# A two-layer transformer kernel: finer loads and a new order in the preamble, and step 0 by halves, in place of an earlier softmax turn in even steps, earlier rows of the second chain and a held-back tile load

## The chip, the cores and the metric

One core of one Trainium2 chip. The metric is the device time of one execution in microseconds; less is better. Three runs of the kernel before gave 1550.05, 1551.38 and 1552.74 us, median 1551.38 us.

## The reference

The input x (1 x 2048 x 448, bf16) goes through two identical layers, with the same weights both times. A layer is a recurrent attention and then a gated feed-forward net (FFN), each behind a layer norm without gain and added to its input:

```
x = x + A(layernorm(x), mem0, Wq, Wk, Wv, Wo)        # 16 heads of 256
x = x + B(layernorm(x), W_gate, W_up, W_down)        # 448 -> 1792 -> 448, relu(gate) * up
(both once more)

A: for each of 64 segments of 32 rows:
    h = concat(mem, xs)                              # 8 + 32 rows
    q, k, v = h Wq, h Wk, h Wv                       # per head
    p = softmax(mask(q k^T / 16))
    o = sum over heads of (p v) Wo
    mem = o[:8]; out rows = o[8:]
```

The 64 segments are a chain: segment s+1 needs the memory rows that segment s left.

## The kernel before, in words

**Two chains.** Layer 1 is chain C1, layer 2 is chain C2; C2 runs six segments (LAG) behind. There are 70 steps. Step g does segment g of C1 and g-6 of C2: steps 0 to 5 hold C1 alone (`single`), steps 6 to 63 hold both (`dual`), steps 64 to 69 hold C2 alone. The 29 even and 29 odd dual steps differ in how their values are gathered: an odd one takes C1's values of x from the step before it, an even one computes them for both chains.

**Folded weights.** The kernel does not form q, k, v. A preamble folds the weights: M = Wk Wq^T per head (`make_M`, 4 heads a call, into `M_sb` and `MT_sb`) and B = Wv Wo per head (`make_B`, 2 heads a call, into `B_sb` and `BT_sb`). For M, Wk and Wq come in transposed by the DMA (`load_T`, line 166, 1024 columns or four heads at a time, 0.92 MB each). For B, Wv comes plain (`load_vo`, lines 177 and 178, 512 columns), TensorE turns it (`turn_B`), and Wo comes plain (line 180). The last two calls, make_B(6) and make_B(7), are made inside step 0. `place(h)` puts heads of even j in the first half of the four-slot groups of `B_sb`, and heads of odd j in the second; so the first part (x = 0) of a `Values` object needs only even j, its second part only odd j.

**A step.** `GPhase` forms G = M h^T in PSUM banks ("gps", evicted by ScalarE and VectorE at line 474). From G come the scores ("S_ps"), then the softmax on VectorE, ScalarE and GpSimd, with its results `Px` and `Pm`. TensorE turns these (`turn_P`, transposes into "PT_ps", copies at line 805). In between `Values` forms h B for the memory (`vm`) and for x (`vx`): a call `both(False)` issues the matmuls over the first 384 features, `both(True)` the tails over the last 64, and whichever comes second ends the sums and evicts them (line 407). The last matmuls ("AT_ps") weigh the values; their first 8 rows per chain are turned ("mps") and become the memory columns of the next step.

**The FFN** of a 128-row tile is cut into ten pieces, queued per chain, and dropped into the steps by `fill` at the hooks inG, mid, before, end and last. The first piece, `turn`, brings the normed rows in turned form to `xnT`, by a DMA transpose (line 315) in dual steps. The normed rows themselves (`rows`, lines 267 and 270, tiles xd_90 and xd_91) are made in `turn` for C1, right behind the first eviction of G by VectorE (`recent["G1"]`). For C2 they are made at the end of the step before, behind the last sum of another tile (`recent["sum"]`, line 349), for the 13 tiles 1 to 13; tile 0 and the tail go C1's way. C1's tiles start in steps with g % 4 = 0, C2's in steps with g % 4 = 2.

**x tiles** live in a ring of six. When C2's FFN has ended a tile, it is stored (line 351), and the tile six further on is queued in `x_next` and loaded by `load_x` (line 366) in the mid hook of a later step.

**Order.** A planner orders instructions by priority and its own costs, but `in_order` ties all TensorE work, and the preamble's loads on SP's queue, to program order. `behind` ties a single instruction behind another on its engine. One PSUM pool of 8 banks, one tag, serves every PSUM tile of the kernel. Buffers of the preamble come in pairs (wk, wq, wv, wo; two tiles wvn).

Of the kernel before, what the change touches and what calls it, by code (L numbers as in the profile page):

```python
# [9 lines left out]
BF = mybir.dt.bfloat16  # L10
# [41 lines left out]
def build_kernel(ctx, tc, A_x, A_mem0, A_Wq, A_Wk, A_Wv, A_Wo, B_W_gate, B_W_up, B_W_down, out,  # L52
# [9 lines left out]
    glob = ctx.enter_context(tc.tile_pool(name="glob", bufs=1))  # L62
    R = min(6, ntiles)
    x_ring = glob.tile([P, R, DM], BF)
    nc.sync.dma_start(x_ring[:, 0:2, :], x_dram[0:256].rearrange("(t p) d -> p t d", p=P))

    def xsl(t):
        return x_ring[:, t % R, :]
# [48 lines left out]
    def in_order(op):  # L117

        eng = op.ins.engine
        if eng in last_of:  # L120
            tc.add_manual_dep(op.ins, last_of[eng],
                              mybir.DependencyInfo(mybir.DependencyClass.NoSync, mybir.DependencyReason.DATA),
                              reason="in_order")
        last_of[eng] = op.ins.name
# [36 lines left out]
    srcs = {n: w.rearrange("d h e -> d (h e)") for n, w in (("k", A_Wk), ("q", A_Wq), ("v", A_Wv))}  # L161
    WoF = A_Wo.rearrange("h (t p) d -> p (h t) d", p=P)

    def load_T(n, i):
        t = bp.tile([P, 8, DM], BF, tag=f"w{n}", name=f"w{n}")
        in_order(nc.sync.dma_start_transpose(t[:], srcs[n][:, 1024 * i:1024 * (i + 1)]))  # L166
        return t

    kq, vo = {}, {}

    def load_kq(i):
        kq[i] = load_T("k", i), load_T("q", i)

    def load_vo(j):

# [53 lines left out]
                              wn[:, dc, 128 * (2 * a + b):128 * (2 * a + b) + 128], ident[:])  # L229
            copy_out(wv[:, 2 * a:2 * a + 2, :], tp[:, :, 0:DM])  # L230

    def make_B(j):

        wv, wo = wv_T.pop(j), vo.pop(j)[1]
        for hh in range(2):
            for mt in range(3):
                ps = psum.tile([P, 512], F32, tag="ps")
                product(ps[:, 0:DM], wv, wo, hh, 128 * mt, 128)
                copy_out(B_sb[:, mt, place(2 * j + hh), :], ps[:, 0:DM], j == 7)
        ps = psum.tile([P, 512], F32, tag="ps")  # L240
        for e, half in enumerate(HALVES):
            product(ps[half, 0:DM], wv, wo, e, 384, 64)
        copy_out(BT_sb[:, place(2 * j), :], ps[:, 0:DM], j == 7)
# [13 lines left out]
    def ln_rows(st, twice=False, after=None):  # L257

        xt, mv, rstd = st
        if twice:  # L260
            xd = xds[n_xn[1] % 2]
            dst, xt = xd[:, :, 0], xt.rearrange("p (k d) -> p k d", d=64)
        else:
            xd = xns[n_xn[0] % 2]
            n_xn[0] += 1
            dst = xd[:, 0:DM]
        behind(nc.vector.tensor_scalar(out=dst, in0=xt, scalar1=mv[:, 0:1], scalar2=rstd[:],
                                       op0=ALU.subtract, op1=ALU.mult), after)
        if twice:
            nc.vector.tensor_copy(xd[:, :, 1], xd[:, :, 0])  # L270
        else:
            nc.vector.tensor_copy(xd[:, DM:DMP], xd[:, 384:DM])
        return xd
# [28 lines left out]
    class FFN:  # L302
# [4 lines left out]
        def norm(self):  # L307
            self.stats = ln_stats(self.t, recent.get("hh"))

        def rows(self, after):  # L310
            self.xn = ln_rows(self.stats, True, after)
            self.xnT = late_sb["xnT"][n_xn[1] % 2]
            n_xn[1] += 1
            if recent["two"]:
                nc.sync.dma_start_transpose(self.xnT[:], self.xn[:].rearrange("p k a b -> p (k a b)"))

        def turn(self):
            if self.xn is None:
                self.rows(recent["G1"])
            if not recent["two"]:  # L320
                tps = psum.tile([P, NCH, P], BF, tag="ps", name="tps")
                for k in range(NCH):
                    transpose(tps[:, k], self.xn[:, k].rearrange("p a b -> p (a b)"), ident[:])
                nc.scalar.copy(self.xnT[:], tps[:])
            self.hh = late_sb["fb"].tile([P, FT, P], BF, tag="hh", name="hh")
# [14 lines left out]
        def down(self, lo, hi):  # L340
            if lo == 0:
                self.dps = psum.tile([P, 512], F32, tag="ps", name="dps")
            ps = self.dps
            for f in range(lo, hi):
                matmul(ps[:, 0:DM], self.hh[:, f, :], late_sb["Wd"][:, f, :], start=(f == 0), stop=(f == FT - 1))
            if hi < FT:
                return
            xt = xsl(self.t)
            recent["sum"] = nc.vector.tensor_tensor(xt, ps[:, 0:DM], xt, op=ALU.add)
            if self.c is C2:  # L350
                nc.sync.dma_start(out_dram[self.t * 128:(self.t + 1) * 128, :], xt)
                t2 = self.t + R
                if t2 < ntiles:
                    x_next.append(t2)

        def pieces(self):
            yield from [self.turn] + [lambda f=f: self.gate_up(f) for f in range(0, FT, 2)] 
            yield from [lambda: self.down(0, 7), lambda: self.down(7, FT)]

    ffn_q = {0: deque(), 1: deque()}  # L360
    x_next = deque()

    def load_x():
        while x_next:
            t = x_next.popleft()
            nc.sync.dma_start(xsl(t), x_dram[t * 128:(t + 1) * 128, :])

    def fill(cid, n):
        for _ in range(n):
# [194 lines left out]
    def single(g, c, inG, mid, soft, before, late, end, last):  # L564
# [67 lines left out]

        alone = g + 1 < LAG if c is C1 else g + 1 < nsteps and (g + 1 - c.lag) % 4 != 0
        soft()
        if not g:
            vm.both(True)
        vm.both(False)
        if odd:
            vox = prev_vom[0]
            v = ahead[g + 1] = x_values(g + 1) if alone else None  # L640
        else:
            v = ahead.pop(g, None)
            if v is None:
                v = x_values(g)
                v.part(0, False)
                v.part(0, True)
            v.part(1, True)
            vox = v.dst
        prev_vom[0] = VOm
        before()  # L650
# [68 lines left out]
    def dual(g, chains, inG, mid, soft, before, late, end, last):  # L719
# [90 lines left out]
        if len(vx) == 2:  # L810
            vx[0].both(False)
            before()
            turn_P()
            vx[0].both(True)
            vx[1].both(True)
            vx[1].both(False)
        else:
            vx[0].part(0, False)
            vx[0].both(True)
            before()  # L820
            turn_P()
            vx[0].part(1, False)
# [59 lines left out]
    def none():  # L882
        pass

    def make_two(j):
        turn_B(j)
        turn_B(j + 1)
        for i in (j, j + 1):
            make_B(i)
            load_vo(i + 2)  # L890

    load_vo(0)
    load_vo(1)
    load_kq(0)
    make_two(0)
    load_kq(1)
    make_M(0)
    tps0 = transposed(mem_in, MEM)
    nc.vector.tensor_copy(mem0T[:], tps0[:, :, 0:MEM])
    set_mem0(C1)  # L900
    for t in range(2):
        prep_stats(C1, t)
        prep_rows(C1, t)
        prep_pe(C1, t)
    make_two(2)
    load_kq(2)
    make_M(1)
    load_kq(3)
    make_two(4)
    if R > 2:  # L910
        in_order(nc.sync.dma_start(x_ring[:, 2:R, :], x_dram[256:R * 128].rearrange("(t p) d -> p t d", p=P)))
    first_G.append(GPhase(0))
    for i in range(2):
        first_G[0].quarter(i)
    make_M(2)
    first_G[0].quarter(2)
    make_M(3)
# [3 lines left out]
    for g in range(nsteps):  # L921
        gb, r = divmod(g, 4)
        if g == LAG:
            set_mem0(C2)
        inG = mid = soft = before = late = end = last = none
        if g == 0:
            def mid():
                turn_B(6)
                turn_B(7)
                make_B(6)  # L930

            def soft():
                make_B(7)
                late_pools()
        elif r == 0:
            def inG():
                fill(0, 1)

            def mid():
                fill(0, 2)  # L940

            def end():
                fill(0, 1)

            def last():
                fill(0, 1)
        elif r == 1:
            def inG():
                prep_stats(C1, gb + 2, recent["G"])

            def mid():
                prep_rows(C1, gb + 2, recent["G"])
                fill(0, 2)

            def before():
                fill(0, 3)
                prep_stats(C2, gb - 1)
                prep_rows(C2, gb - 1)

            def end():  # L960
                prep_pe(C1, gb + 2)
                fill(1, 1)
                prep_pe(C2, gb - 1)

            def last():
                fill(1, 1)
        elif r == 2:
            def inG():
                fill(1, 1)

            def mid():
                fill(1, 1)

            def end():
                fill(1, 1)

            def last():
                fill(1, 1)
        else:
            def mid():  # L980
                fill(1, 1)
                load_x()

            def before():
                fill(1, 1)

            def end():
                fill(1, 1)

            def last():  # L990
                fill(1, 1)
        step(g, inG, mid, soft, before, late, end, last)
        for c in (C1, C2):
            t, j = divmod(g - c.lag, 4)
            if j == 3 and 0 <= t < ntiles:
                f = FFN(c, t)
                f.norm()
                if c is C2 and recent["two"] and g + 1 < nseg and t:
                    f.rows(recent["sum"])
                ffn_q[c.cid].extend(f.pieces())  # L1000
    fill(1, 20)

# [52 lines left out]
```

## Time and profile before

| | |
|---|---|
| Median of 3 runs | 1551.38 us |
| The profiled execution: time, span | 1551.38 us, 1549.6 us |
| Granted TensorE clock, mean | 0.999 |
| TensorE (PE) busy | 1515.6 us, 98% |
| VectorE (DVE), ScalarE (ACT), GpSimd (POOL) busy | 910.5, 625.7, 148.2 us |
| Step 0 begins (mask matmul) | 65.47 us |
| Step 1's first G matmul | 83.50 us |
| Chain that ended last | 92% PE, 2% DMA, 2% DVE, 2% SP's queue |

Times in the profile are microseconds from the span's start unless marked ns. "PEld" is TensorE loading weights, "SPq" a DMA issue on SP's queue. In a line of the timeline stand the start, the duration, engine, source line, operation, out<-in and count. A DMA's issue is not its landing.

### The profile page before, as it was taken

To read this page: it belongs to the slowest core of one execution; us is meant where nothing else is said; L and a number is where in the kernel's file an instruction comes from. 1 tells how busy PE (TensorE), PEld (TensorE's weight loads), DVE (VectorE), ACT (ScalarE), POOL (GpSimd) and SP (SyncE) were. 2 spreads that over 40 slices of the span, in tenths; PEclk is the share of its full clock that TensorE was granted. 3 is DMA by queue.
4 is the path that set the end of the run, shared out by engine and by line. 5 is a ranking of instruction groups with operands and counts; after the bars stand their busy time and mean duration, and the time that the engine had idled before them with its cause. 6 is when DMAs were issued, how large, how long until landed. Compare 5 with 4: busy or idle time off the path is not lost.

```text
span 1549.6 us, 82294 instructions
## 1 busy us (share of the span) xinstructions
PE 1515.6 (98%) x38579; PEld 1141.7 (74%) x38579; DVE 910.5 (59%) x2085; ACT 625.7 (40%) x1459; POOL 148.2 (10%) x384
## 2 busy tenths in 40 slices
PE   7999999999999999999999999999999999999998
PEld 4566777778777777777778777877777787777775
DVE  5535466665656566556656566565656665656543
ACT  5634344434344343434434343434434343444333
POOL 2001011010101001010001101010100100001000
PEclk9999999999999999999999999999999999999999
DMA  9731000010000000000000101001000000000000
GB/s 238 161 91 44 5 11 15 10 21 12 10 15 16 17 12 19 12 21 6 14 17 12 21 10 21 12 12 14 16 17 12 17 12 14 10 7 14 5 8 9
DMA packets 83636, 39.20 MB, mean 25 GB/s; under 512 B 65752, under 2 KB 82400, under 8 KB 83296
## 3 DMA queue, kind: packets, MB, share of 16 engines
q1 hardware_dynamic: 83264, 33.94, 10.3%
q8 instruction: 301, 4.93, 1.3%
q14 instruction: 39, 0.32, 0.1%
q10 hardware_dynamic: 32, 0.01, 0.0%
HBM read 14.00 MB, written 1.84 MB: 10 GB/s over the span
## 4 chain that ended last, share of the span: by engine, by line
PE 92%; DMA 2%; DVE 2%; SPq 2%; ACT 1%; issue 0%; POOL 0%; POOLq 0%; ACTq 0%
PE gps L127 30%; PE vps L127 28%; PE gate L127 11%; PE AT_ps L127 7%; PE dps L127 6%; PE S_ps L127 5%; PE PT_ps L130 2%; SPq L166 1%; DMA wq<-in_A_Wq_dram 1%; DMA xnT_1184<-xd_91 1%; PE up L127 1%; PE ps L127 1%; PE mps L127 1%; PE tps L130 0%; DVE G L474 0%
## 5 line engine op out<-in xcount | busy, mean ns | idle before, releaser
L127 PE MATMUL gps<-hTr,M_sb 128*128 128x80 bf16 (+1 forms) x11760 | 414.7, 198 | 0.0
L127 PEld LDWEIGHTS <-M_sb 128*128 128x128 bf16 x11760 | 405.3, 99 | 4.4
L474 DVE CAST G<-gps 128x480 bf16<-128x480 f32 (+2 forms) x327 | 194.0, 611 | 222.1 <-PE gps L127 221.4
L474 ACT CAST G<-gps 128x480 bf16<-128x480 f32 (+2 forms) x327 | 165.6, 525 | 350.7 <-PE gps L127 350.7
L127 PEld LDWEIGHTS <-hTr 128*32 128x32 bf16 (+3 forms) x8000 | 177.3, 93 | 142.2 <-issue 42.2
L127 PE MATMUL vps<-B_sb,hTr 128*32 128x448 bf16 x4464 | 234.2, 353 | 0.0
L127 PEld LDWEIGHTS <-Wgu 64*128 64x128 bf16 x6272 | 181.0, 94 | 21.8 <-issue 13.0
L407 ACT CAST VOm<-vps 128x448 bf16<-128x448 f32 x251 | 121.5, 529 | 124.5 <-PE vps L127 124.4
L407 ACT CAST vox<-vps 128x448 bf16<-128x448 f32 x186 | 96.1, 533 | 93.4 <-PE vps L127 89.6
L337 DVE SCALAR_TENSOR_TENSOR hh<-gate,ut 128x256 bf16<-128x256 f32 x224 | 94.7, 423 | 66.4 <-ACT ut L336 66.3
L407 DVE CAST vox<-vps 128x448 bf16<-128x448 f32 x186 | 112.8, 619 | 27.4 <-PE vps L127 25.0
L336 ACT CAST ut<-up 128x256 bf16<-128x256 f32 x224 | 83.8, 374 | 64.8 <-PE up L127 64.8
L127 PE MATMUL up<-xnT_1183,Wgu 64*128 64x128 bf16 x1568 | 104.0, 216 | 0.0
L127 PE MATMUL gate<-xnT_1183,Wgu 64*128 64x128 bf16 x1568 | 103.9, 216 | 0.0
L127 PE MATMUL gate<-xnT_1184,Wgu 64*128 64x128 bf16 x1568 | 99.3, 216 | 2.9 <-DMA xnT_1184<-xd_91 1.8
L127 PE MATMUL up<-xnT_1184,Wgu 64*128 64x128 bf16 x1568 | 99.3, 216 | 0.0
L127 PE MATMUL gps<-hTr,MT_sb 64*128 64x80 bf16 (+1 forms) x3920 | 91.5, 195 | 4.4 <-ACT hTr L693 2.1
L127 PE MATMUL dps<-Wd,hh 128*128 128x448 bf16 x448 | 92.7, 353 | 0.0
L127 PE MATMUL S_ps<-G,hTr 128*8 128x320 bf16 (+3 forms) x2048 | 86.2, 299 | 2.1 <-DVE G L474 1.7
L127 PEld LDWEIGHTS <-MT_sb 64*128 64x128 bf16 x3920 | 76.4, 96 | 15.2 <-issue 7.6
L127 PE MATMUL vps<-B_sb,memTp_80 128*32 128x448 bf16 x1680 | 85.7, 352 | 0.0
L127 PE MATMUL vps<-B_sb,memTp_78 128*32 128x448 bf16 x1680 | 85.7, 352 | 0.0
(163 smaller groups left out, 1607.0 us busy)
## 6 DMA issues: line engine op xcount, KB each, us to landing
wo<-in_A_Wo_dram SPq DMA_DIRECT2D x8, 448.0 KB, 5.4
out_dram<-x_ring SPq DMA_DIRECT2D x16, 112.0 KB, 1.7
Wgu<-in_B_W_gate_dram SPq DMA_DIRECT2D x7, 224.0 KB, 3.5
Wgu<-in_B_W_up_dram SPq DMA_DIRECT2D x7, 224.0 KB, 3.4
Wd<-in_B_W_down_dram SPq DMA_DIRECT2D x7, 224.0 KB, 2.7
wvn_124<-in_A_Wv_dram SPq DMA_DIRECT2D x4, 384.0 KB, 3.7
wvn_125<-in_A_Wv_dram SPq DMA_DIRECT2D x4, 384.0 KB, 6.2
x_ring<-in_A_x_dram SPq DMA_DIRECT2D x10, 112.0 KB, 2.8
```

The costliest lines, as they stand in the source:

```text
L127: in_order(nc.tensor.matmul(*a, **k))
L130: in_order(nc.tensor.transpose(*a))
L166: in_order(nc.sync.dma_start_transpose(t[:], srcs[n][:, 1024 * i:1024 * (i + 1)]))
L336: recent["ut"] = nc.scalar.copy(ut[:], gu[1][:])
L337: recent["hh"] = nc.vector.scalar_tensor_tensor(out=self.hh[:, f:f + 2, :], in0=gu[0][:], scalar=0.0, in1=ut[:], op0=ALU.max, op1=ALU.mult)
L407: op = self.evac[2 * x + e](self.dst[:, 2 * e + x, :], self.ps[x][e][:, 0:DM])
L474: op = (cp_a, cp_v)[self.side](gp.G[:, self.side, self.t0:self.t0 + self.n, gp.c0:gp.c1, :], self.ps[:, 0:self.n * gp.NP].rearrange("p (m ...
```

## The change

Preamble:

- `load_kq` fetches each four heads of Wk and Wq in four DMA transposes of two heads (k, q, k, q; 0.46 MB each) in place of two of four heads. The order of the plain loads between them stays the same.
- The first two tiles of x are loaded behind the first Wk and Wq, no longer first of all.
- `turn_B(j + 1)` moves in between the two heads of make_B(j); the first turn of each pair is called ahead of `make_two`.
- The four quarters of the first G start earlier: the first ahead of make_two(4), the second behind it.
- make_B(6) and the turn of 7 move behind step 0's scores. Step 0 computes the first halves (x = 0) of its values of memory and x together, and then the second halves.

Steps:

- Even dual steps issue the tails of both chains' values ahead of `turn_P`, no longer behind it.
- C2's normed rows are made in `turn`, behind the first eviction of G in the next step, as for C1.
- The load of the next x tile is issued right behind the store of the finished one.

```diff
-    nc.sync.dma_start(x_ring[:, 0:2, :], x_dram[0:256].rearrange("(t p) d -> p t d", p=P))
...
-    def load_T(n, i):
-        t = bp.tile([P, 8, DM], BF, tag=f"w{n}", name=f"w{n}")
-        in_order(nc.sync.dma_start_transpose(t[:], srcs[n][:, 1024 * i:1024 * (i + 1)]))
-        return t
...
     def load_kq(i):
-        kq[i] = load_T("k", i), load_T("q", i)
+        kq[i] = [bp.tile([P, 8, DM], BF, tag=f"w{n}", name=f"w{n}") for n in "kq"]
+        for h in range(2):
+            for n, t in zip("kq", kq[i]):
+                c = 1024 * i + 512 * h
+                in_order(nc.sync.dma_start_transpose(t[:, 4 * h:4 * h + 4], srcs[n][:, c:c + 512]))
...
-    def make_B(j):
+    def make_B(j, between=None):
         wv, wo = wv_T.pop(j), vo.pop(j)[1]
         for hh in range(2):
+            if hh and between:
+                between()
...
-        def rows(self, after):
-            self.xn = ln_rows(self.stats, True, after)
+        def turn(self):
+            self.xn = ln_rows(self.stats, True, recent["G1"])
             self.xnT = late_sb["xnT"][n_xn[1] % 2]
             n_xn[1] += 1
             if recent["two"]:
                 nc.sync.dma_start_transpose(self.xnT[:], self.xn[:].rearrange("p k a b -> p (k a b)"))
-        def turn(self):
-            if self.xn is None:
-                self.rows(recent["G1"])
-            if not recent["two"]:
+            else:
...
-            recent["sum"] = nc.vector.tensor_tensor(xt, ps[:, 0:DM], xt, op=ALU.add)
+            nc.vector.tensor_tensor(xt, ps[:, 0:DM], xt, op=ALU.add)
             if self.c is C2:
                 nc.sync.dma_start(out_dram[self.t * 128:(self.t + 1) * 128, :], xt)
                 t2 = self.t + R
                 if t2 < ntiles:
-                    x_next.append(t2)
+                    nc.sync.dma_start(xsl(t2), x_dram[t2 * 128:(t2 + 1) * 128, :])
...
         soft()
-        if not g:
-            vm.both(True)
-        vm.both(False)
+        if g:
+            vm.both(False)
+        else:
+            v = ahead[0] = x_values(0)
+            for x in range(2):
+                vm.part(x, True)
+                v.part(x, True)
+                vm.part(x, False)
+                if not x:
+                    v.part(0, False)
...
-            v.part(1, True)
+            if g:
+                v.part(1, True)
...
             vx[0].both(False)
             before()
-            turn_P()
             vx[0].both(True)
             vx[1].both(True)
+            turn_P()
             vx[1].both(False)
...
+    def load_x(lo, hi):
+        in_order(nc.sync.dma_start(x_ring[:, lo:hi, :], x_dram[lo * 128:hi * 128].rearrange("(t p) d -> p t d", p=P)))
     def make_two(j):
-        turn_B(j)
-        turn_B(j + 1)
-        for i in (j, j + 1):
-            make_B(i)
-            load_vo(i + 2)
+        make_B(j, lambda: turn_B(j + 1))
+        make_B(j + 1)
+    first_G.append(GPhase(0))
     load_vo(0)
     load_vo(1)
     load_kq(0)
+    load_x(0, 2)
+    turn_B(0)
     make_two(0)
+    load_vo(2)
+    load_vo(3)
     load_kq(1)
     make_M(0)
+    turn_B(2)
...
     make_two(2)
+    load_vo(4)
+    load_vo(5)
     load_kq(2)
     make_M(1)
     load_kq(3)
+    turn_B(4)
+    first_G[0].quarter(0)
     make_two(4)
+    load_vo(6)
+    load_vo(7)
     if R > 2:
-        in_order(nc.sync.dma_start(x_ring[:, 2:R, :], x_dram[256:R * 128].rearrange("(t p) d -> p t d", p=P)))
-    first_G.append(GPhase(0))
-    for i in range(2):
-        first_G[0].quarter(i)
+        load_x(2, R)
+    first_G[0].quarter(1)
     make_M(2)
...
             def mid():
                 turn_B(6)
-                turn_B(7)
-                make_B(6)
             def soft():
-                make_B(7)
+                make_two(6)
                 late_pools()
...
                 fill(1, 1)
-                load_x()
...
-                if c is C2 and recent["two"] and g + 1 < nseg and t:
-                    f.rows(recent["sum"])
```

More of the change, by code (lines that the diff above doesn't have):

```diff
@@ L360, in build_kernel @@
     ffn_q = {0: deque(), 1: deque()}
[L361 to L366, printed above, removed]
     def fill(cid, n):
```

## The prediction

> **What bounds the kernel now.** I read the page first. TensorE (PE) is busy 98% of the span and PE is 92% of the chain that ended last, so outside the preamble nothing but a PE stall taken away, or a new one, can move the time.
>
> ```profile
> PE 1515.6 (98%) x38579; PEld 1141.7 (74%) x38579; DVE 910.5 (59%) x2085; ACT 625.7 (40%) x1459; POOL 148.2 (10%) x384
> ...
> DMA  9731000010000000000000101001000000000000
> ```
>
> The DMA row is high only in the first two slices (of 38.7 us). So I read the chain of waits up to step 0. Columns: start, duration, what.
>
> ```profile
> 11.37 5.88 DMA wq<-in_A_Wq_dram
> ...
> 27.37 6.22 DMA wq<-in_A_Wq_dram
> ...
> 42.34 7.45 DMA wq<-in_A_Wq_dram
> ...
> 49.93 5.60 PE ps L127 x32
> ...
> 57.84 5.45 PE ps L127 x32
> ```
>
> Until 49.8 us the chain is SP's queue and the landings of Wq. SP's part of the timeline shows each load issued within 0.2 us of the one before: the loads are one stream. The fourth Wq is issued at 51.09 and lands 6.54 us later by the trace, at 57.63; the last make_M starts at 57.69. So PE meets the stream's end there too: **the stream sets the start of step 0**, whatever PE did earlier. That makes the stream's rate the thing to know; the table by stretches gives it (second column from the end: DMA share; last: GB/s).
>
> ```profile
> 10.50:12.50 2.00, 2.00 (x11) 1.00 (x9) 0.87 (x2) 0.97 (x2) 0.00 (x0) 1.00 1.28 291
> 12.50:14.50 2.00, 2.00 (x13) 0.78 (x12) 1.96 (x5) 1.28 (x3) 0.00 (x0) 1.00 0.94 214
> 28.50:30.50 2.00, 2.00 (x12) 0.88 (x10) 1.64 (x3) 1.26 (x3) 0.00 (x0) 1.00 0.74 146
> 43.25:45.25 2.00, 2.00 (x14) 0.85 (x13) 1.38 (x3) 1.32 (x3) 0.00 (x0) 1.00 1.31 131
> 48.25:50.25 2.00, 1.79 (x60) 1.55 (x59) 0.90 (x2) 0.39 (x1) 0.00 (x0) 1.00 1.03 190
> 53.75:55.75 2.00, 1.76 (x13) 0.63 (x11) 1.31 (x5) 1.82 (x5) 0.00 (x0) 1.00 1.28 288
> ```
>
> Inside a transpose 290 GB/s flow. The other five rows each hold a place where one DMA transpose follows another. There 214, 146, 131, 190 and 288 flow: 2 x (290 - rate) / 290 = 0.52, 0.99, 1.10, 0.69 and 0.01 us lost, mean 0.66. (An instruction fetch falls into the third; the fifth follows a fetch that had held the stream, so the next transpose was ready.)
>
> Last, PE's waits from 200 to 1440 us: the steady steps have almost none.
>
> ```profile
> PE gate L127 <- DMA xnT_1184<-xd_91: 1.8, 3, 0.9
> PE gps L127 <- ACT hTr L853: 0.7, 2, 0.4
> ```
>
> **The change part by part.** The sum is made against the profiled execution, 1551.38 us (span 1549.6), which is also the median of the runs shown. About 0.2%, 3.1 us, is what a measurement of this kernel can tell from no change.
>
> *Wk and Wq in halves.* Each set of four heads now has three places where a transpose follows a transpose, before one: 8 more up to the last Wq. At 0.66 each the stream ends **5.3 us** later. Bounds: 0.01 each (0.1 us), if half a transpose waits ready in the queue, as in the fifth row; 0.99 each (7.9). The queue's depth can be read: the issue of the second Wk ends at 27.33 and its data flow until about 28.8, 1.5 us, as for the other seven. That is a little less than half a transpose (0.46 MB at 290 GB/s is 1.58 us), so the next issue still starts only about 1.5 us before the data run out, as now; I keep the mean. The Trainium skill speaks against this edit. Its page "DMA: Bandwidth & Descriptors", section "Rules for kernel authors", asks for 1 MiB or more per DMA, and its "Latency and other measured facts" puts a DMA's fixed cost at about 2 us; if all of that showed at each of the eight places, an estimate from the page would be 16 us in place of 5.3, and the rows above show no place that dear.
>
> *The last half.* When the last Wq's second half lands, the first half of make_M(3) is done. Of its 32 matmuls the first two heads have 12, in 5.6 us: 12 x 0.175 = **2.1 us** come off the path. It needs PE to be waiting there, and it is: make_M(2)'s rest 3.5, quarter 2 some 1.9, make_M(3)'s first half 2.1 make 7.5 us, while the two halves of the last Wk and Wq take 1.83 MB / 290 = 6.3 plus four gaps of 0.66, 8.9.
>
> *Earlier turns, earlier products, earlier quarters, x later.* Nothing: PE waits for Wk and Wq 3.1 us and for Wv 6.8 before, and the stream's total bytes do not change. SP is passed by x (one issue of 0.46 us, 0.23 MB), which it only exchanges with other loads. x lands near 19 us; stats, POOL's two steps and rows (about 2.5 us in all) are due at PE near 23, and a miss would be covered by the wait for the second Wq near 36. Without that cover it would cost 1 to 2 us. The later loads of Wv and Wo reach step 0 on time: Wv of 6 lands 3.7 us behind its issue at 55.69, moved to about 61, and step 0 starts near 68.
>
> *Step 0.* The wait of PE for BT_sb, 0.69 us at 75.49, goes, since the products with even j (3.1 us) now lie over ScalarE's last copies; one more switch between full and tail matmuls costs 0.1. **-0.6**, with bounds 0 and -0.7. Moving make_B(6) puts three copies among the softmax on VectorE; the softmax result is at hand 5 us before its use (74.6 against 79.8), which hides it.
>
> *turn_P behind the tails, 29 even dual steps.* The timeline of one:
>
> ```profile
> 705.40 0.36 PE L130 MATMUL PT_ps<-ident,Pm_110 104*128 104x104 bf16 x4
> ...
> 705.69 0.95 PE L127 MATMUL vps<-BT_sb,hTr 64*32 64x448 bf16 x32
> ...
> 706.13 1.16 DVE L407 CAST vox<-vps 128x448 bf16<-128x448 f32 x2
> 706.17 0.97 ACT L407 CAST vox<-vps 128x448 bf16<-128x448 f32 x2
> 706.57 0.75 PE L127 MATMUL vps<-B_sb,hTr 128*32 128x448 bf16 x12
> ```
>
> Single starts in the trace put the first Pm transpose 0.111 us behind the last Px one, against 0.045 in odd steps: a wait for POOL of 0.066 us, 1.9 us in 29 steps. It goes. The switches of kind on PE cost the same in both orders (0.285 + 0.139 + 0.279 against 0.282 + 0.281 + 0.139). What comes: a wait for PSUM. C1's values hold 4 banks and C2's take the other 4 with their tails, so the two banks of PT_ps are had only when C1's first sums are evicted. By these rows an eviction starts 0.44 us after the first tail and takes 0.53 (ACT) or 0.62 (DVE), plus 0.06 until PE sees it: 1.03 or 1.12. PE is there after 0.60 + 0.28 = 0.88. So 0.15 to 0.24 us, 4.4 to 7.0 in 29 steps, less 1.9: 2.5 to 5.1. I take **+3.8**; the low bound is -1.9, if a bank should be free. Behind the turn nothing is late: C2's last 48 matmuls (2.46 us) cover the copies of 0.5.
>
> *C2's rows in turn, 13 tiles.* Rows and copy (0.50 + 0.29 on DVE) move from 691.42 to behind the first DVE eviction of G, which ends at 693.69: transpose issued near 694.5 in place of 692.31, first gate matmul at 698.16. That margin of 3.66 us is C1's now (735.68 to 739.35). Trace starts show C1's gate late by 0.27, 0.59, 0.59 and 1.11 us in 4 of 14 tiles, where the landing took over 3.6 us: 0.18 a tile, x 13 = **+2.4**. Bounds 0 and 5: C2's transposes land in 2.9 to 4.5 us, as C1's do. POOL's rstd is done by then.
>
> *x load behind the store.* It waits on SP for the store's landing (1.7 us, 691.53 to 693.2), issues in 0.53 and is through before the transpose queued behind it at 694.5: 0. If the store takes its longest, 3.5 us, that tile's transpose is 1.1 us late; that lies within the upper bound above.
>
> Sum: 5.3 - 2.1 - 0.6 + 3.8 + 2.4 = +8.8 us. **1560.2 us.**
>
> **The rivals.**
>
> *Halves without gaps (faster).* If a half waits ready in the queue, as at 53.75, the stream ends where it does now: -2.1 - 0.6; no bank wait gives -1.9, and C2's rows half their price, +1.2. That is -3.4: 1548.0 us. It decides where a gap costs under 0.2 us. For it: the fifth row. Against it: the other four, and the issue that ends 1.5 us before the data.
>
> *The preamble comes out even (no change).* At 0.34 us a gap, the eight take 2.7 and give 2.7 back; with banks free in even steps (-1.9) and C2 at 2.4 the sum is +0.5: 1551.9. It takes two of my terms wrong at a time.
>
> *Queue order (slower still).* If SP's x load stands before C2's transpose and stretches its landing to the longest seen, 4.5, in the ten tiles that load, 0.85 x 10 comes on top of the main sum less the 1.8 already counted for ten: +15.5, 1566.9. Against it: the store two thirds of a microsecond ahead of C2's transpose now, whose landings (median 3.4) are as C1's.
>
> **How the numbers follow.** The main case has 0.6, with a range of its own from 1554.5 to 1565: gaps of 0.33 to 0.9, bank wait 2.5 to 5.1, C2 1 to 4. Halves without gaps 0.13, even 0.17, queue order 0.1. 8 in 10 lie from 1549.5 to 1566. Faster by over 0.2% is most of the first rival: 0.11. Within 0.2%: 0.19, from the second rival and the edges. Slower by over 0.2%: 0.70.
>
> **What would show it.** Step 0's mask matmul near 68 us in place of 65.47; 16 transposes of Wk and Wq with GB/s dips at each border; PE waiting for Wq before the second halves; no wait for BT_sb in step 0. In even steps, a gap of about 0.45 us between the last tail and the first transpose where now 0.28 stands for such a switch; gate waits on both xnT tiles. The prediction is wrong if the stream ends by 58 us, or if even steps show no gap at PT_ps.

## The result, and the profile after

The changed kernel takes 1558.24 us (median of 6 runs, 1556.38 to 1559.12), the kernel before 1552.06 in the 6 runs beside them: ratio 1.0037 [1.0024, 1.005], 6.2 us slower. The forecast was +8.8, the time inside its range. The profiled execution took 1558.49 us with a span of 1556.7, 7.1 us more than the span before. Where the 7.1 us lie is read from the starts of the same matmuls in both traces:

| start, us | before | after | difference |
|---|---|---|---|
| last Wq lands | 57.63 | 59.09 | +1.46 |
| step 0's mask matmul | 65.47 | 67.81 | +2.34 |
| step 1's first G matmul | 83.50 | 85.02 | +1.52 |
| step 7's | 183.56 | 183.49 | -0.07 |
| step 63's | 1419.02 | 1425.91 | +6.89 |
| step 69's | 1520.98 | 1528.09 | +7.11 |

Both profiles hold one stretch of 3.4 us in which TensorE was granted half its clock, some 1.7 us lost; before it lies at 162.1, after at 21.2, so at step 7 both have had theirs. **Up to step 7 these two traces are level. The whole 7 us between them come from the dual steps.** There, even steps are longer by a median of 0.09 us (22.42 for 22.33 where g % 4 = 0, 21.60 for 21.51 where it is 2; 29 of them: 2.6 us), C2's gate matmuls are late by 4.04 us in sum (0.01 before) and C1's by 3.01 (2.57 before): 2.6 + 4.0 + 0.4 = 7.0.

The page of after: TensorE as busy as before, and the DMA row again high in the first two slices alone.

```profile
PE 1516.1 (97%) x38579; PEld 1139.1 (73%) x38579; DVE 909.2 (58%) x2085; ACT 625.8 (40%) x1459; POOL 148.9 (10%) x384
...
DMA  9731000000000001010010000000000000000000
```

The chain of waits of after, up to step 0 (start, duration, what). Before, it held landings of Wq, the last of them from 42.34 on; now it holds none:

```profile
13.29 1.55 SPq L171
14.89 5.21 DMA x_ring<-in_A_x_dram
20.13 0.63 DVE stats L250
20.76 1.05 DVE B_sb L189 x2
...
24.30 2.62 DVE M_sb L189 x6
...
29.76 1.31 PE ps L126 x6
...
60.19 5.45 PE ps L126 x32
```

The chain goes over the landing of x, then VectorE, and from 29.76 on over PE with VectorE's and ScalarE's copies between. TensorE's waits up to 84.8 us (waited for, total us, times, longest) give the price, in the first of these lines:

```profile
PE ps L126 <- DVE B_sb L189: 4.6, 1, 4.6
PE tp L129 <- DMA wvn_123<-in_A_Wv_dram: 4.5, 2, 4.4
```

The half clock at 21.2 us is this wait's: in the table by stretches (clock: third column from the end), TensorE stands still in the first stretch and has half its clock in the second.

```profile
17.80:21.20 3.40, 0.00 (x0) 0.00 (x0) 1.07 (x3) 0.00 (x0) 0.00 (x0) 1.00 1.01 312
21.20:24.60 3.40, 3.27 (x9) 1.28 (x9) 3.40 (x9) 0.53 (x1) 0.79 (x2) 0.51 1.29 270
```

VectorE's timeline shows why a copy to `B_sb` was late by 4.6 us. It executes in order; x's first statistics stood ahead of two finished sums of make_B in its queue, and waited 6.98 us for x:

```profile
20.13 0.63 DVE L250 BATCH_NORM_STATS2 stats<-x_ring 128x6 f32<-128x448 bf16 x1 [6.98 <-DMA x_ring<-in_A_x_dram]
20.67 1.14 DVE L189 CAST B_sb<-ps 128x448 bf16<-128x448 f32 x2
```

The wait for Wq (3.1 us before) and that for `BT_sb` in step 0 (0.7) are gone. The table by stretches around seven of the thirteen borders between half transposes (columns as before: DMA share next to last, GB/s last):

```profile
10.00:12.00 2.00, 2.00 (x20) 1.64 (x18) 1.18 (x3) 1.02 (x2) 0.00 (x0) 1.00 0.91 207
12.00:14.00 2.00, 2.00 (x13) 0.79 (x12) 1.01 (x2) 1.37 (x4) 0.00 (x0) 1.00 1.27 283
14.00:16.00 2.00, 2.00 (x14) 0.75 (x12) 0.00 (x0) 1.48 (x3) 0.00 (x0) 1.00 0.89 189
28.30:30.30 2.00, 1.76 (x24) 1.22 (x22) 2.00 (x10) 1.10 (x3) 0.45 (x3) 1.00 1.27 288
45.00:46.40 1.40, 1.40 (x21) 1.18 (x19) 0.96 (x2) 0.92 (x2) 0.00 (x0) 1.00 1.26 285
48.40:50.40 2.00, 2.00 (x12) 0.88 (x9) 1.50 (x3) 1.35 (x3) 0.00 (x0) 1.00 1.26 206
50.50:52.50 2.00, 2.00 (x62) 1.51 (x63) 0.93 (x3) 0.92 (x2) 0.00 (x0) 1.00 1.20 220
```

Four of the seven have a gap (2 x (290 - rate) / 290 = 0.57, 0.70, 0.58 and 0.48 us), three lost 0.05 us or less: 0.34 in the mean. An instruction fetch of 8 KB falls into the third of the four. From the landing of the last Wq the eight added borders cost 1.46 / 8 = 0.18 us each, but that difference of two traces also holds where the instruction fetches fell in each.

An even dual step of after (the turn of the softmax is now behind the 32 tails):

```profile
707.13 0.95 PE L126 MATMUL vps<-BT_sb,hTr 64*32 64x448 bf16 x32
...
707.61 0.97 ACT L398 CAST vox<-vps 128x448 bf16<-128x448 f32 x2 [1.97 <-PE vps L126]
708.19 0.34 PE L129 MATMUL PT_ps<-ident,Px_108 104*128 104x104 bf16 x4
708.38 0.35 PE L129 MATMUL PT_ps<-ident,Pm_109 104*128 104x104 bf16 x4
```

From the last tail's start to the first transpose's, 0.461 us pass in single starts, where before 0.285 passed from the matmul ahead of the turn, and from the last Px transpose to the first Pm one 0.046, for 0.113. ScalarE's first eviction takes 0.53 us and ends at 708.14; the turn starts 0.05 later. TensorE's waits from 200 to 1440 us now name both xnT tiles:

```profile
PE gate L126 <- DMA xnT_1191<-xd_89: 3.3, 4, 1.5
PE gate L126 <- DMA xnT_1192<-xd_90: 2.3, 4, 0.8
```

### The profile page after: what moved, and what is told of

Read it like the earlier page. It is cut to its first block, busy times and chain, and to the rows that moved or that the text cites. A ratio compares the mean times of both kernels' runs of the same rounds, so it can differ in the third digit from the quotient of the medians.

```text
span 1556.7 us, 82306 instructions
## 1 busy us (share of the span) xinstructions
PE 1516.1 (97%) x38579; PEld 1139.1 (73%) x38579; DVE 909.2 (58%) x2085; ACT 625.8 (40%) x1459; POOL 148.9 (10%) x384
## 4 chain that ended last, share of the span: by engine, by line
PE 91%; DVE 4%; DMA 3%; SPq 1%; ACT 1%; issue 0%; POOL 0%; POOLq 0%; ACTq 0%
PE gps L126 29%; PE vps L126 27%; PE gate L126 11%; PE AT_ps L126 7%; PE dps L126 6%; PE S_ps L126 5%; PE ps L126 2%; PE PT_ps L129 2%; DVE vox L398 1%; DMA xnT_1192<-xd_90 1%; DMA xnT_1191<-xd_89 1%; PE up L126 1%; SPq L171 1%; PE mps L126 1%; PE tps L129 0%
```

## The experiments

Ratios are to the kernel before, in runs on the same chip; the kernel before had medians of 1552.53, 1552.36 and 1551.0 us in the three groups. The 0.2% bound of the prediction is wider than some of the intervals below, so they are given each time.

### The preamble and step 0 alone

The changed kernel with the three edits of the dual steps taken back (`turn_P` ahead of the tails, `rows` behind `recent["sum"]`, `x_next` held back to the mid hook):

```diff
-        def turn(self):
-            self.xn = ln_rows(self.stats, True, recent["G1"])
+        def rows(self, after):
+            self.xn = ln_rows(self.stats, True, after)
...
             before()
+            turn_P()
             vx[0].both(True)
             vx[1].both(True)
-            turn_P()
...
+                if c is C2 and recent["two"] and g + 1 < nseg and t:
+                    f.rows(recent["sum"])
```

> The preamble and step 0 as changed; the even steps, C2's rows and the x reload as in the kernel before. Theory (the loss is made in the steady steps: the PSUM wait and the later transposes of C2): step 1 begins within 1 us of 83.5 once a half-clock stretch is allowed for, no gap beyond 0.29 us ahead of PT_ps, gate waits on C1's xnT alone, and a time within 2 us of the kernel before, 5 to 8 us below the changed one. Rival of the prediction's sum (the finer stream costs 2.6 us in all): 2 to 3 us above the kernel before. The 4.6 us wait of PE for VectorE's B_sb stays in both.

1553.84 us, median of 12: 1.001 [1.0001, 1.0018], some 4 us below the changed kernel (ratios 1.001 and 1.0037). C2's lateness is back at 0.01, the gap before PT_ps at 0.285. The wait for `B_sb` stays (4.7 us). The half clock comes with it again, from 19.7 us on, while TensorE stands still. So the dual steps carry most of the loss, and the preamble and step 0 the rest, 0.2 to 2.8 us; that interval does not decide between the theory's "within 2 us" and the rival's 2 to 3.

### x first again

The changed kernel, with `load_x(0, 2)` ahead of all other loads:

```diff
+    load_x(0, 2)
     load_vo(0)
...
     load_kq(0)
-    load_x(0, 2)
```

> The changed kernel with the first two x tiles loaded first of all again. Theory (VectorE's queue stands at the statistics of an x that has not landed, with B_sb's evictions behind it): the wait of 4.6 us goes, make_M(0) starts as Wq lands, step 0 begins 1.5 to 3 us earlier than in the changed kernel without a half-clock stretch (66.1), the time falls by 1.5 to 3 us. Rival (the stream of loads sets step 0 whatever PE waited for before): the wait goes, but step 0 begins within 0.5 us of 66 and the time stays.

1558.54 us, median of 6: 1.0037 [1.0024, 1.005], the changed kernel's ratio. The 4.6 us wait is gone from TensorE's waits, and the one for Wq is back:

```profile
PE tp L129 <- DMA wvn<-in_A_Wv_dram: 5.7, 2, 5.4
PE ps L126 <- DMA wq<-in_A_Wq_dram: 4.0, 4, 1.4
```

The last Wq lands at 59.68 and step 0's mask matmul follows 5.83 later, at 65.51. TensorE's last wait for Wq ends at 52.24, with the third set's second half, and it comes to the last one 0.3 us behind its landing: loads and TensorE are level there. Step 0 begins 2.3 us earlier than in the changed kernel, and the lead holds to the end of the steps (step 69 at 1525.83 for 1528.09). Then this profile loses most of it: it has no half clock in the preamble, but one near the end, behind a stretch in which TensorE was busy for less than half the time:

```profile
1539.80:1543.20 3.40, 1.55 (x20) 0.95 (x19) 1.42 (x3) 0.91 (x1) 0.55 (x1) 0.95 0.10 34
1543.20:1546.60 3.40, 3.40 (x74) 3.40 (x71) 0.59 (x2) 0.74 (x2) 0.00 (x0) 0.54 0.00 0
```

My theory's 1.5 to 3 us are there at step 0 and not in the time, where the rival's "unchanged" stands; with 0.13% to either side of each ratio, 2 us can hide between them.

### x's statistics behind make_M(0)

x still loads late; the statistics are tied behind VectorE's last copy of make_M(0), so that nothing of make_B stands behind them:

```diff
-            nc.vector.tensor_copy(dst, src)
+            recent_copy[0] = nc.vector.tensor_copy(dst, src)
...
     make_M(0)
+    m0_copy = recent_copy[0]
...
-        prep_stats(C1, t)
+        prep_stats(C1, t, m0_copy)
```

> The changed kernel, x loaded late as in it, but VectorE's statistics of the first two tiles ordered behind VectorE's last copy of make_M(0). Theory (it is the order in VectorE's queue, not x's landing): the 4.6 us wait at B_sb goes though x lands at 20 us as before; PE waits at most 2 us for the normed rows later; step 0 as in the run with x first, within 0.7 us. Rival (the landing of x itself is what PE needs): PE waits 3 us or more at the transposes of xn.

1560.06 us, median of 6: 1.0049 [1.0037, 1.0061]. The waits of TensorE up to 84.8 us:

```profile
PE tp L129 <- DMA wvn<-in_A_Wv_dram: 4.1, 1, 4.1
PE tps L129 <- DVE xn L269: 2.9, 1, 2.9
...
PE tps L129 <- DVE xn L274: 0.6, 1, 0.6
```

The 4.6 us wait is gone, so VectorE's order did cause it. But TensorE now waits 2.9 + 0.6 us for the normed x itself. Late x costs TensorE 4.6 us in the one order of VectorE and 3.5 in the other; the order alone is not the cause. That is the rival's sign, and step 0 begins at 66.76, 1.3 us behind the run with x first, where the theory allowed 0.7.

### The preamble alone, with x first

Both of the above: the dual steps of before, the new preamble, x first.

```diff
+    load_x(0, 2)
     load_vo(0)
...
     load_kq(0)
-    load_x(0, 2)
```

> The changed preamble with x first, and the steady steps of the kernel before. Theory: both losses are gone; the last half of Wq lands 1 to 2 us later than in the kernel before, of which 2.1 come back in make_M(3), and step 0 gives 0.9: 1 to 3 us below the kernel before, 1549 to 1551. Rival (the finer stream eats its gain): no gain, within 1 us of the kernel before.

1550.76 us, median of 12: 0.9989 [0.998, 0.9998]. It is the only kernel whose interval lies below the kernel before, and the best of those I ran on that reading. Its chain up to step 0:

```profile
44.44 6.62 DMA wq<-in_A_Wq_dram
...
51.20 3.34 PE ps L126 x20
...
56.84 5.45 PE ps L126 x32
...
64.54 0.24 PE S_ps L126
```

Behind the last landing (58.77) stand 5.70 us up to step 0's mask matmul (64.47), in place of 65.47 - 57.63 = 7.84: make_M(3) starts at 56.69, ahead of that landing, and the last half of it saves 2.14. TensorE does not wait for this half: the chain leaves the loads at 51.06, where the third set's Wq has landed, and stays on TensorE and its evictions from there. Against the preamble with late x, step 0 starts 2.5 us earlier, step 69 3.2 (1519.08 for 1522.28), and the median is 3.1 less. The pair before this one gave 2.3 at step 0 and nothing in the median, from 6 runs each. I take x first to be worth some 2 us, on four starts of each kind below.

### turn_P behind the tails, alone

```diff
             before()
-            turn_P()
             vx[0].both(True)
             vx[1].both(True)
+            turn_P()
```

> The kernel before with one edit: even dual steps turn P behind the tails of both chains. Theory (PSUM banks: the two of PT_ps are had when ScalarE and VectorE have evicted C1's first sums): 0.46 us ahead of PT_ps in place of 0.28, 0.046 between Px and Pm in place of 0.11, so 0.09 to 0.12 us longer for each of 29 steps, 2.6 to 3.3 us in all. Rival (it only moves the wait for GpSimd): no gap beyond 0.29, 1.9 us faster.

1554.49 us, median of 12: 1.0016 [1.0005, 1.0026], 2.1 us by the medians and 2.5 by the ratio. The gap is 0.461, even steps take 22.42 and 21.60, just as in the changed kernel, and C2's gates are on time (0.01). The timeline of one step:

```profile
706.05 0.97 ACT L407 CAST vox<-vps 128x448 bf16<-128x448 f32 x2 [1.97 <-PE vps L127]
706.63 0.34 PE L130 MATMUL PT_ps<-ident,Px 104*128 104x104 bf16 x4
```

Again 706.05 + 0.53 for the first eviction is 706.58, and the turn starts at 706.63.

### C2's rows in turn, alone

```diff
-        def rows(self, after):
-            self.xn = ln_rows(self.stats, True, after)
+        def turn(self):
+            self.xn = ln_rows(self.stats, True, recent["G1"])
...
-                if c is C2 and recent["two"] and g + 1 < nseg and t:
-                    f.rows(recent["sum"])
```

> The kernel before with one edit: C2's normed rows are made in turn, in 13 tiles; the x reload stays in its later hook. Theory (margin of 3.66 us against landings of 2.9 to 4.5): transposes of C2 issued 3.7 us behind the first G matmul of their step in place of 1.5; C2's gates late in about 4 of 13 tiles, 2 to 3 us in all, and the time 2 to 3 us longer. Rival (the loss needs the x load in the queue): C2's gates late by under 1 us in all.

1556.6 us, median of 8: 1.0028 [1.0014, 1.0042], 4.2 us. C2's gates are late by 4.45 us in sum. TensorE's waits from 200 to 1440 us, first line:

```profile
PE gate L127 <- DMA xnT<-xd: 5.5, 7, 1.5
```

Right in kind, and above the 2 to 3 us that I gave it. But the run does not put the rival to the test, for the x load stands ahead of the transpose here too:

```profile
869.71 0.36 SPq L347 DMA_DIRECT2D out_dram<-x_ring  x1
873.27 0.34 SPq L362 DMA_DIRECT2D x_ring<-in_A_x_dram  x1
873.72 1.25 SPq L315 DMA_TRANSPOSE xnT<-xd  x1
```

Most transposes of C2 are issued 3.7 us behind the first G matmul of their step; this one comes at 4.76, and the one at 783 at 3.89. So 1.2 of the 4.45 us are the wait for the store, and the other 3.2 come from landings of over 3.6 us. No run shows the late rows without the load ahead of the transpose.

### The x load behind the store, alone

```diff
-                    x_next.append(t2)
+                    nc.sync.dma_start(xsl(t2), x_dram[t2 * 128:(t2 + 1) * 128, :])
...
-                load_x()
```

> The kernel before with one edit: the next x tile is loaded right behind the store. Rows of C2 stay early, so their transpose has 5.8 us. Theory: no wait at C2's gates, step lengths as before, span within 1 us of the kernel before apart from a half-clock stretch. Rival (queue order): the load waits for the store's landing ahead of the transpose and makes it 1 to 3.5 us later in some tiles, but C2's margin still covers all but 1 us in all.

One run, 1550.22 us (span 1548.4): nothing lost, C2 late by 0.02 in sum, C1 by 2.16. While the rows are made early, the load costs nothing. It does not test the queue order either: the transpose is issued ahead of the load here (867.53 and 869.74 in one tile), not behind it.

### turn_P between the tails

The changed kernel, with the turn after C1's tails and ahead of C2's, so that it asks for its two PSUM banks while four are still free:

```diff
             vx[0].both(True)
-            vx[1].both(True)
             turn_P()
+            vx[1].both(True)
```

> The changed kernel with turn_P between the tails of C1 and those of C2. Then four banks are still free when PT_ps is asked for. Theory (banks): 0.28 us ahead of PT_ps, the bare switch, in place of 0.46; one more pair of switches costs 0.28, so an even step is 0.1 us longer than in the changed kernel. Rival (TensorE waits there for the softmax or for the tails' results, not for banks): 0.4 us or more ahead of PT_ps, as it comes 0.4 us earlier than in the changed kernel.

One run, 1558.66 us. The timeline:

```profile
707.62 0.57 PE L126 MATMUL vps<-BT_sb,hTr 64*32 64x448 bf16 x16
708.12 0.36 PE L129 MATMUL PT_ps<-ident,Px 104*128 104x104 bf16 x4
```

The gap falls from 0.461 to 0.282, the value of a switch of kind alone. With the instructions unchanged and only C2's tails moved behind it, the 0.18 us wait is gone: it was a wait for PSUM banks, of which C2's tails take the last four. Even steps take 22.38 and 21.55, 0.05 shorter than in the changed kernel, where I had expected 0.1 longer for the added switch of kind; I had over-counted that switch.

### The halves alone

```diff
-        kq[i] = load_T("k", i), load_T("q", i)
+        kq[i] = [bp.tile([P, 8, DM], BF, tag=f"w{n}", name=f"w{n}") for n in "kq"]
+        for h in range(2):
+            for n, t in zip("kq", kq[i]):
+                c = 1024 * i + 512 * h
+                in_order(nc.sync.dma_start_transpose(t[:, 4 * h:4 * h + 4], srcs[n][:, c:c + 512]))
```

> The kernel before with one edit: Wk and Wq in halves. Theory from the runs so far (a seam between two transposes costs 0.15 to 0.26 us, as the stream ends 1.1 to 2.1 us later in them): last Wq lands at 58.8 to 59.7 in place of 57.63, step 0 begins 5.7 us behind it, at 64.5 to 65.4 in place of 65.47; the time within 1 us of the kernel before, rather below it. Rival (the prediction's 0.66 a seam): last Wq at 62.9, step 0 near 68.6, 3 us slower.

1551.68 us, median of 11: 1.0 [0.999, 1.001]. The last Wq lands at 56.95, 0.68 earlier than before in spite of eight more borders. A price of 0.66 a border has fallen. Step 0's mask matmul is at 64.14, 1.3 us earlier than in the profile of before; the times don't show it, and the next paragraphs tell how far one such start can be trusted.

### Whole transposes, and only the last set halved

Two kernels on the best one: first all sets whole, then only the fourth in halves.

```diff
-        for h in range(2):
-            for n, t in zip("kq", kq[i]):
-                c = 1024 * i + 512 * h
-                in_order(nc.sync.dma_start_transpose(t[:, 4 * h:4 * h + 4], srcs[n][:, c:c + 512]))
+        for n, t in zip("kq", kq[i]):
+            c = 1024 * i
+            in_order(nc.sync.dma_start_transpose(t[:], srcs[n][:, c:c + 1024]))
```

> The changed preamble and step 0 with x first and Wk and Wq whole, steady steps as before. Theory: the last Wq lands at 57.6 as before and the whole make_M(3) follows, so step 0 begins at 65.2 to 65.6; step 0 itself gives 0.8 to 0.9; 0.9 us below the kernel before in all, 1 us above the run of the changed preamble with x first. Rival (the new order of turns, products and quarters is what moves step 0): step 0 near 64.5 here too.

1550.15 us, median of 11: 0.9996 [0.9987, 1.0005]. Step 0's mask matmul at 65.31, last Wq at 57.00.

```diff
-        for h in range(2):
+        m = 2 if i == 3 else 1
+        for h in range(m):
...
-                c = 1024 * i + 512 * h
-                in_order(nc.sync.dma_start_transpose(t[:, 4 * h:4 * h + 4], srcs[n][:, c:c + 512]))
+                w, c = 1024 // m, 1024 * i + 1024 // m * h
+                in_order(nc.sync.dma_start_transpose(t[:, 8 // m * h:8 // m * (h + 1)], srcs[n][:, c:c + w]))
```

> As the run of the changed preamble with x first, but only the last four heads come in halves. Theory (only the last half is worth anything, each seam costs): two seams more than before in place of eight, last Wq at 57.9 to 58.2, step 0 at 63.6 to 63.9; 0.6 to 0.9 us better than with all in halves, about 2.5 us below the kernel before. Rival (PE needs the halves of the earlier sets as well): step 0 no earlier than 64.5.

1551.31 us, median of 11: 0.9998 [0.9989, 1.0007]. Expected 0.6 to 0.9 us better than with all sets halved; not seen. TensorE's wait for Wq (2.9 us up to 34.2) brought half the clock there, and step 0's mask matmul is at 67.20.

The times don't tell these preambles apart. The profiles also hold four runs of one and the same preamble, that of before (before itself, turn_P alone, rows alone, x load alone): their mask matmuls are at 65.47, 67.01, 66.15 and 66.61, so a single start is good to 1.5 us at best. By groups, step 7's first G matmul comes at 182.9 in the mean of these four (182.45 to 183.56); at 183.4 in the four with the new preamble and late x (182.38 to 184.76); at 180.9 in the four with x first (179.93 to 182.16). So late x makes the new preamble level with the old one, or half a us worse, and x first makes it 2 us better, which is what the medians say too (1.001 and 0.9989 of the kernel before). Part of it is the half clock: ahead of step 7 the four with late x hold five stretches of 3.4 us with it, the four with x first one. At 1.7 us each that is up to 1.7 of the 2.4 us between these two groups. How much of the 2 us the halves bring stays open: whole transposes with x first came to step 7 at 180.56, halves with the rest as before at 180.64.

### Which tiles are late: the instruction fetch moved

In the profiles, tiles whose transposed rows landed late mostly had a packet of 8 to 16 KB on the instruction queue in flight. To move the fetches and leave the steps as they are, 64 idle TensorE transposes of the identity were put at the start of the kernel with C2's rows in turn:

```diff
+    idle = psum.tile([P, 8, P], BF, tag="ps", name="idle")
+    for i in range(64):
+        transpose(idle[:, i % 8], ident[:], ident[:])
```

> The run with C2's rows in turn, plus 64 transposes of the identity at the very start, where PE waits for Wv (their result is not used). Theory (a landing over 3.6 us is one whose data meet an instruction fetch; the fetch's place follows the count of PE's instructions): step times as there, but the tiles whose gates are late are others: not those at 604, 694, 783 and 874 us for C2. Rival (the tile's addresses or its own queue decide): the same four tiles are late by about the same 0.6, 0.8, 1.2 and 1.6 us.

One run, 1558.14 us. C2's lateness is as large as without them, 4.30 us for 4.45, in other tiles: with C2's rows in turn alone the main four were at 604, 694, 783 and 874 us, now they are at 252, 342, 432, 1051 and 1141, while the four old ones land in 2.92 to 3.02 us. In this run a packet of instructions began 1.2 to 2.3 us behind the issue of each of the five late transposes, and none did between 0.85 and 2.5 us behind the four old ones. A tile's own addresses or place in the ring can't do that; the place of the fetch in the instruction stream does.

## Why the prediction was right or wrong

**Direction and mechanism of the main loss: right.** The dual steps were to cost 6.2 us (turn 3.8, rows 2.4) and cost 7.0 in the profile. The signs foretold in "What would show it" came: a gap of 0.46 us for the foretold 0.45, gate waits on both tiles, no wait for `BT_sb`, the mask matmul at 67.8 for 68. The last agrees for the wrong reasons: the wait for `B_sb` and the half clock behind it, in place of the stream. Two signs did not come: TensorE did not wait for Wq ahead of the second halves, and three of the seven borders above have no dip.

**turn_P: right, somewhat too dear.** Its parts: bank wait 0.461 - 0.285 = 0.176 us (foretold 0.15 to 0.24), POOL's wait gone, 0.067 (0.066). That leaves 0.109 a step; steps grew by 0.09. The sum took the middle of the range, 0.131 net, where the lower end applied: ScalarE's eviction (0.53 us), not VectorE's (0.62), freed the first banks. 2.6 us in the profile, 2.1 to 2.5 by its own runs, for 3.8.

**C2's rows and the x load: 4.0 for 2.4 and 0.** C1's lateness a tile was carried over, 0.18 x 13, and that part came: landings of over 3.6 us made 2.7 us of the 4.0. The step that failed is the "0" for the x load. It waits for the store and stands ahead of the transpose on SP's queue; I costed it at nothing because a typical store lands in 1.7 us. In the worst tile the store took 3.2:

```profile
871.29 0.36 SPq L348 DMA_DIRECT2D out_dram<-x_ring  x1
874.48 0.34 SPq L351 DMA_DIRECT2D x_ring<-in_A_x_dram  x1
874.93 1.25 SPq L316 DMA_TRANSPOSE xnT_1191<-xd_89  x1
```

Three tiles (transposes at 696, 785 and 875) went that way. The others are issued 3.72 us behind the first G matmul of their step, these three 0.49, 0.14 and 0.67 us later, 1.3 in all. This is the queue-order rival in small, in three tiles rather than ten. Which tiles a fetch hits is chance of place: it is set by the instruction count, and 13 more tiles now had no slack for a hit.

**The stream: wrong, 1.46 us for 5.3.** The step that failed is "That is a little less than half a transpose ... I keep the mean". That mean came from borders of whole transposes, one of them with an instruction fetch in it; the seven borders of halves above give 0.34, with 0.05 or less at three of them, near its lower bound of 0.01. The issue of about 1.5 us ahead, 0.43 MB, nearly covers a half of 0.46 MB, which would explain the free borders: behind SP's row at 9.32, issued in 1.68 us, the border lost 0.05. Why four others lost 0.48 to 0.70 us is not shown. Over the profiles, the last Wq landed at 56.5 to 59.2 us with whole sets (mean of six 57.7) and at 56.9 to 59.8 with halves (mean of seven 59.0): 1.3 us for eight borders, 0.16 each. The whole sets alone scatter over 2.7 us, and the halves alone landed at 56.95, so 0.16 is no more than a rough figure. The Trainium skill's 2 us a DMA ("DMA: Bandwidth & Descriptors", "Latency and other measured facts") would by the prediction's estimate have made it 16; queued back to back, these transposes show 0.16 to 0.34 a border, about a sixth of it or less, and the measurement decides.

**x later: wrong, "nothing" was 4.6 us of waiting.** The step that failed is "a miss would be covered by the wait for the second Wq near 36". I looked for the miss at TensorE's use of x alone. It came on VectorE, whose queue stood at the statistics with make_B's evictions behind them, and it used up that cover: in the changed kernel step 0 begins 8.7 us behind the last Wq, not the 5.7 and 5.8 of the two runs of halves with x first. And a wait of 4.6 us brought half the clock for 3.4 us behind it, a cost that I had not thought of. By the groups of starts above, late x costs 2.4 us at step 7, up to 1.7 of them by the half clock.

**The last half: the size right, its condition wrong.** With x first make_M(3) starts 1.95 and 2.08 us ahead of the last landing and the half saves its 2.1. The step that failed is "It needs PE to be waiting there, and it is": in the changed kernel TensorE comes to make_M(3) at 60.03, 0.94 behind the landing at 59.09, so there the half saves nothing. In the trace before, too, TensorE came to the last make_M straight from quarter 2 (57.69 for the landing at 57.63); the stream did bind in two other runs of that preamble (59.23 for 59.19, 58.37 for 58.33).

**Step 0: right**, 18.03 to 17.21 us, -0.82 for -0.6.

Up to step 7 the sum was to be 5.3 - 2.1 - 0.6 = +2.6; it was -0.07 between the two traces and +0.5 between the groups: two misses, the stream 4 us too dear and x at nothing for 2.4 (the last half's gain lost in it), partly cancelled. That the total is only 2.6 us too high is in part luck, and this excess is the preamble's; the steps were put 0.8 too low. The first rival was nearer on the stream and had the steps wrong. Taken one at a time the parts add up to 0.10 + 0.16 + 0.28 = 0.54% where the whole is 0.37 [0.24, 0.5]; by these intervals they may still add up.

## What to carry to other kernels

Before a transfer is moved later, list what stands behind its first consumer on that engine's in-order queue, not only who needs its data: the miss shows up where an unrelated eviction waits. A matmul group that takes the last PSUM banks should not be put ahead of a small one that needs a bank too; ask at each switch how many banks are held and when the oldest is evicted. Work made as early as possible for a DMA is slack against landings that vary; taking 2.2 us of it away cost nothing at a median landing and 4 us in the sum of the late ones, 1.3 of them because a load that waited for a store had come to stand ahead on the same queue.

## What the runs showed of the hardware that I had not expected

- **Instruction fetches delay DMA transposes in flight.** Over 14 profiles of 28 transposes each, 142 landed more than 3.6 us after their issue; in 106 of these a packet of the instruction queue began 0.85 to 2.5 us after the issue. Of the 250 on time only 29 had one. The median landing of those on time is 2.9 us, of all 3.2, the longest in the changed kernel 4.6. The run with the idle transposes, which moved the fetches, moved the late tiles.
- **The issue of a DMA transpose ends about 1.5 us before its data do** (27.33 and about 28.8 for the second Wk of the kernel before). At 290 GB/s that is an estimated 0.43 MB standing ready. Size alone does not decide what a border costs: between halves of 0.46 MB the seven rows lost 0.01 to 0.70 us, between wholes of 0.92 MB the five of the prediction 0.01 to 1.10.
- **A short wait of TensorE can cost half its clock for 3.4 us behind it.** Ten of the 14 profiles have such stretches, and each follows a stretch of 3.4 us in which TensorE was busy for 68% or less; all four with late x and the new preamble have it behind the stall. In the profile of before:

```profile
158.70:162.10 3.40, 2.31 (x57) 1.71 (x56) 1.38 (x6) 1.04 (x4) 0.90 (x3) 1.00 0.05 13
162.10:165.50 3.40, 3.40 (x57) 3.40 (x54) 0.66 (x1) 0.56 (x2) 0.00 (x0) 0.51 0.00 0
```

The Trainium skill ("TensorE: Matmul & The Clock Gate", "What's actually happening") has a free-running window of 3413 ns, after which an idle TensorE falls to half its clock. The length agrees, and so does the free running: the two stretches in the run with the idle transposes begin at 18.28 and 1544.04, 447 windows of 3413 ns apart. That the window need not be idle throughout is what these lines add. Which gap draws the half clock stays open: on the same grid the wait of 2.6 us at 31 falls into two windows with TensorE busy for 2.12 us each, less than the 2.31 above, and neither drew it.
